# A fixed list of steps for the first chunk of an attention and feed-forward kernel

## The chip, the cores and the metric

One Trainium2 chip, one of its cores. The metric is the device time of one execution in microseconds (us). TensorE (PE; PEld is its weight load), VectorE (DVE), ScalarE (ACT), GpSimd (POOL) and SyncE (SP, which issues all transfers) each run their own queue in order and wait for each other by semaphores.

## What is computed

Local attention with a summary of every block, then a maxout layer, then a bilinear layer:

```python
def _attn_ref(q, k, v):                    # (2, 8, 768, 64)
    block, window = (32, 16)
    k_sum = k.reshape(B, H, nb, block, D).max(axis=3)
    v_sum = v.reshape(B, H, nb, block, D).mean(axis=3)
    scores_l = scale * np.matmul(q, k.transpose(0, 1, 3, 2))   # kept where |i - j| < window
    scores_s = scale * np.einsum('bhsd,bhnd->bhsn', q, k_sum) + np.log(block)
    ...                                    # softmax over both, times [v, v_sum]
def _moe_ref(x, w1, w2, w3, w_out):        # x (1536, 512), d_ff 768
    h = np.maximum(np.maximum(x @ w1, x @ w2), x @ w3)
    return (h @ w_out).astype(np.float32)
def _moe2_ref(x, w_a, w_b, w_out):         # d_ff 1536
    return ((x @ w_a) * (x @ w_b) @ w_out).astype(np.float32)
```

## The kernel before

The 1536 tokens are four chunks of 384 (three tiles of 128). Attention is worked per group `g`: one chunk and one pair of heads `p`, so groups 0 to 3 make chunk 0, groups 4 to 7 make chunk 1. For a group there are, in turn: keys copied into their layout with the block maxima spread between them (`key_parts`, L159); for each of three tiles the scores (`scores`: two products on PE, L251; mask and row minimum on DVE, L257; exponentials on ACT, L258); the normalisation (`normal`: sums to ACT, L273, reciprocal on DVE, L274, scaling on POOL, L276); the transposes of the result (`transposes`: PE L289, out of PSUM by DVE L293 for two tiles and ACT L295 for the third); the values with their block means (`spread`, L180; the means are spread on DVE, L191), turned by PE and copied out by ACT (`turned`, L210 and L211); and the product with the values (`values`, L308), which leaves PSUM split in two halves, a rounded one (ACT, L518) and its rest (DVE, L519). Here this last product of group 3 is called **M3**, its two halves make the fourth slice of chunk 0's `x`.

After that come dense layers: `layers12` multiplies each chunk's `x` with 18 weight tiles (12 products `ph` of 384 columns for each, three products for each of four slices, L514) and so on; `layers34` follows. These products are the bulk of PE's work.

Every 128x512 weight tile, here **w0**, **w1**, ... in the order of loading, comes as 64-bit words and is taken apart by `w_round` and `w_parts`: a scaling `psw` (ACT L444 or DVE L442), the low words (ACT L446), shift and sign (DVE L448, L449), an addition (POOL L450), then a rounded half (ACT L454) and its rest (POOL or DVE, L455). A tile is of use when both halves stand.

What sets the order: SP's transfers go out in program order (its queue is scheduled by hand), eight at most under way, since each waits for the one eight places earlier to land. The other engines' order is set when the program is built, by a scheduler that knows dependencies, priorities and the `issue_after` pins. PE's instructions of the first chunk are pinned one behind the other (`chain`); DVE, ACT and POOL are pinned at a few places only (`behind_all`). `opening` (L317) writes the first chunk's steps, `turn_over` puts products of zeros between them that nothing reads.

Of the kernel before, what the change touches and what calls it, by code (L numbers as in the profile page):

```python
# [19 lines left out]
P = 128  # L20
# [10 lines left out]
NSEG, PAD = S // HALF + 1, HALF - WINDOW  # L31
# [24 lines left out]
W64, W32, WBUFS, QB, FB, SM, GB, BANKS = (4, 3), (4, 3), (24, 10), 4, (9, 1), 2, (12, 9), (2, 2, 1, 2, 2)  # L56
# [7 lines left out]


# [11 lines left out]
def attention_then_maxout_then_bilinear(ctx: ExitStack, tc: tile.TileContext, qt, kt, vt, vwin, wall, const, out):  # L77
# [4 lines left out]
    V, A, G, T = nc.vector, nc.scalar, nc.gpsimd, nc.tensor  # L82
# [67 lines left out]
    def keys(b, p):  # L150

        row = w64_p.tile([P, NSEG * HALF], F32, tag=f"full{b}", name="row", bufs=FB[b])
        nc.sync.dma_start(out=row, in_=kt[b, p][:, P - WINDOW - PAD:])
        if b == 0:
            raw["k", p] = row
        else:
            key_parts(b, p, row)

    def key_parts(b, p, row):  # L159

        kk = k_t[p].rearrange("p (m k) -> p m k", k=SEG)
        row_k = row.rearrange("p (m k) -> p m k", k=HALF)
# [16 lines left out]

    def spread(b, p, full):  # L180

        z = Z_AT[0]
        mean = sm_p.tile([P, 1, NB], F32, tag="mean", name="mean")
        V.tensor_reduce(mean, full.rearrange("p (o n k) -> p o n k", o=1, k=BLOCK), AX.X, ALU.add)
        if b == 0:
            vs = sm_p.tile([P, VSEG, SEG], F32, tag="vs", name="vs")
            G.memset(vs[:, 0, 0:PAD], 0.0)
            G.tensor_copy(vs[:, 0, PAD:HALF], full[:, 0:WINDOW])
            G.tensor_copy(vs[:, 1:VSEG, 0:HALF],
                          full[:, WINDOW:WINDOW + (VSEG - 1) * HALF].rearrange("p (m k) -> p m k", k=HALF))  # L190
            V.tensor_scalar(vs[:, :, HALF:SEG], mean.to_broadcast([P, VSEG, NB]), 1.0 / BLOCK, None, ALU.mult)  # L191
            v_s[p] = vs.rearrange("p m k -> p (m k)")
            return
        ps = ps_t.tile([NB, P], F32, tag="t", name="psvs")
        T.transpose(ps, mean[:, 0], ident)
# [4 lines left out]
    def turned(p):  # L200

        n, vs = SIZES[0], v_s.pop(p)
        for i0 in range(0, n, 2):
            i1 = min(n, i0 + 2)
            ps = ps_t.tile([NC, 2, 2, P], F32, tag="t", name="psvt")
            with chain():
                for i in range(i0, i1):
                    for a in range(2):
                        k0 = (2 * i + a) * SEG + HALF - Z_AT[a]
                        marks["pe"] = T.transpose(ps[:, i - i0, a], vs[:, k0:k0 + NC], ident).ins  # L210
            A.activation(v_t[p][:, i0:i1].rearrange("k i a h d -> k i a (h d)"), ps[:, 0:i1 - i0], AF.Copy)  # L211
# [26 lines left out]
    def scores(g, i):  # L238
# [3 lines left out]
        if i == 0:  # L242
# [5 lines left out]
        with chain(g <= NP) if g <= NP else behind_all("first"):  # L248
# [3 lines left out]
            if g <= NP:  # L252
                marks["pe"] = ins
        for a in range(2):
            mask = cst[:, MASK[t, a]:MASK[t, a] + NC]

            marks["scores", g, i] = V.tensor_tensor_reduce(s[:, a], ps[:, a], mask, -1.0 / D ** 0.5, 3e38, ALU.add, ALU.min, nm[:, a:a + 1]).ins  # L257
            A.activation(s[:, a], s[:, a], AF.Exp, bias=nm[:, a:a + 1], scale=-1.0, accum_out=sm[:, a:a + 1])  # L258
        if g == 0:
            turn_over(TURN[1])  # L260
# [7 lines left out]
    def normal(g):  # L268
# [5 lines left out]
        last[0] = V.reciprocal(r, r).ins  # L274
        s, r = s.rearrange("p i a k -> p (i a) k"), r.rearrange("p i a o -> p (i a) o")
        marks["normal", g] = G.tensor_tensor(s, s, r.to_broadcast([P, 2 * n, NC]), ALU.mult).ins  # L276

    def transposes(g):
        at, n = exps.pop(g)[0], CHUNKS[groups[g][0]][2]
        a_t[g] = aT = sm_p.tile([NC, MAXT, 2, P], F32, tag="aT", name="aT")  # L280
        for i0 in range(0, n, 2):
            i1 = min(n, i0 + 2)
            ps = ps_t.tile([NC, 2, 2, P], F32, tag="t", name="pst")
            if g < NP and i0 == 0:
                turn_over(TURN[2])
# [6 lines left out]
            if AT_DVE[g >= len(groups) // 2][i0 // 2 % 2]:  # L292
                marks["aT", g] = V.tensor_copy(aT[:, i0:i1], ps[:, 0:i1 - i0]).ins  # L293
            else:
                A.activation(aT[:, i0:i1], ps[:, 0:i1 - i0], AF.Copy)  # L295

    def values(g):
# [13 lines left out]
        if g == NP - 1:  # L311
            marks["first"] = ins
        split(x_t[c, p], ps[:, 0:n * P], V)
# [3 lines left out]
    def opening():  # L317

        def spread_(p, i):
# [493 lines left out]
```

## Time and profile before

| | |
|---|---|
| Median of 3 runs | 550.48 us (550.28 to 551.54) |
| The profiled execution | 550.42 us |
| Its span in the trace | 548.6 us |
| PE busy | 538.7 us (98%) |
| DVE, ACT, POOL busy | 384.3, 271.3, 200.4 us |
| Read from HBM | 48.09 MB |

The page gives busy time per engine, the chain of work that ended last, and the costliest groups of instructions. All times in the trace count from the span's start.

### The profile page before, as it was taken

To read this page: it belongs to the slowest core of one execution; us is meant where nothing else is said; L and a number is where in the kernel's file an instruction comes from. 1 tells how busy PE (TensorE), PEld (TensorE's weight loads), DVE (VectorE), ACT (ScalarE), POOL (GpSimd) and SP (SyncE) were. 2 spreads that over 40 slices of the span, in tenths; PEclk is the share of its full clock that TensorE was granted. 3 is DMA by queue.
4 is the path that set the end of the run, shared out by engine and by line. 5 is a ranking of instruction groups with operands and counts; after the bars stand their busy time and mean duration, and the time that the engine had idled before them with its cause. 6 is when DMAs were issued, how large, how long until landed. Compare 5 with 4: busy or idle time off the path is not lost.

```text
span 548.6 us, 8994 instructions
## 1 busy us (share of the span) xinstructions
PE 538.7 (98%) x3364; PEld 513.0 (93%) x3364; DVE 384.3 (70%) x804; ACT 271.3 (49%) x660; POOL 200.4 (37%) x176
## 2 busy tenths in 40 slices
PE   7899999999999999999999999999999999999997
PEld 7789999999999999999999989989998998998986
DVE  5798975785422641739888997986997798574464
ACT  4699765586542422534675545634544542440130
POOL 3479997362210121313414432421621452230120
PEclk9999999999999999999999999999999999999999
DMA  8991831674100002213303042131122121000014
GB/s 306 365 291 73 270 132 67 224 227 129 61 1 1 1 5 111 76 40 116 115 1 115 17 144 72 40 115 58 58 78 76 39 78 39 1 0 1 0 48 184
DMA packets 17131, 51.81 MB, mean 94 GB/s; under 512 B 2112, under 2 KB 2752, under 8 KB 17088
## 3 DMA queue, kind: packets, MB, share of 16 engines
q1 hardware_dynamic: 17088, 51.25, 28.0%
q8 instruction: 26, 0.43, 0.3%
q14 instruction: 17, 0.14, 0.1%
HBM read 48.09 MB, written 3.15 MB: 93 GB/s over the span
## 4 chain that ended last, share of the span: by engine, by line
PE 88%; DVE 5%; issue 1%; ACT 1%; POOL 1%; POOLq 0%; DVEq 0%; ACTq 0%
PE ph L514 24%; PE qb L514 17%; PE qg L514 9%; PE py L514 8%; PE po L683 6%; PE po L684 6%; PE po L682 6%; PE qd L514 4%; PE ps L251 3%; PE psv L308 2%; PE pst L289 2%; DVE wt L455 1%; DVE w L448 1%; POOL t L650 1%; DVE w L449 1%
## 5 line engine op out<-in xcount | busy, mean ns | idle before, releaser
L514 PE MATMUL ph<-x,wt 128*128 128x384 f32 x864 | 156.9, 337 | 0.0
L514 PEld LDWEIGHTS ph<-x,wt 128*128 128x128 f32 x864 | 149.2, 188 | 0.4
L450 POOL TENSOR_TENSOR w<-w,w 128x512 int32<-128x512 int32 x60 | 82.5, 1378 | 161.9 <-DVE w L449 82.8
L514 PE MATMUL qb<-yt,wt 128*128 128x384 f32 x576 | 110.6, 335 | 0.3 <-ACT s L633 0.3
L514 PEld LDWEIGHTS qb<-yt,wt 128*128 128x128 f32 x576 | 101.1, 188 | 1.4 <-ACT s L633 0.6
L518 ACT ACTIVATE hg<-t 128x384 fp32r<-128x384 f32 x72 | 37.0, 521 | 72.1 <-DVE t L542 40.8
L650 POOL TENSOR_TENSOR t<-t,ca 128x384 f32<-128x384 f32 x36 | 44.1, 1241 | 64.4 <-DVE t L649 64.3
L514 PE MATMUL qg<-yt,wt 128*128 128x384 f32 x288 | 58.0, 334 | 0.0
L683 PE MATMUL po<-wt,hg 128*128 128x512 f32 (+1 forms) x146 | 56.6, 387 | 0.0
L684 PE MATMUL po<-wt,hg 128*128 128x512 f32 (+1 forms) x146 | 56.5, 387 | 0.0
L682 PE MATMUL po<-wt,hg 128*128 128x512 f32 (+1 forms) x146 | 56.5, 387 | 0.0
L696 DVE TENSOR_TENSOR acc<-po,acc 128x512 f32<-128x512 f32 (+1 forms) x61 | 40.7, 678 | 21.7 <-PE po L684 21.7
L542 DVE TENSOR_TENSOR t<-ph,t 128x384 f32<-128x384 f32 x48 | 26.4, 552 | 40.2 <-PE ph L514 33.9
L514 PE MATMUL py<-hg,wt 128*128 128x384 f32 x288 | 53.8, 339 | 0.4 <-ACT hg L518 0.4
L514 PEld LDWEIGHTS qg<-yt,wt 128*128 128x128 f32 x288 | 50.7, 188 | 0.0
L514 PEld LDWEIGHTS py<-hg,wt 128*128 128x128 f32 x288 | 49.5, 188 | 0.9 <-ACT hg L518 0.7
L258 ACT ACTIVATE s<-s,nm 128x120 f32<-128x120 f32 x96 | 37.0, 388 | 21.5 <-DVE nm L257 21.0
L444 ACT ACTIVATE w<-w 128x512 f32<-128x512 f32 x30 | 20.2, 675 | 50.6 <-DMA w<-wall 49.6
L454 ACT ACTIVATE wt<-w 128x512 fp32r<-128x512 f32 (+1 forms) x60 | 34.9, 582 | 19.1 <-POOL w L450 9.8
L519 POOL TENSOR_TENSOR hg<-t,hg 128x384 fp32r<-128x384 f32 x23 | 25.0, 1092 | 51.2 <-ACT hg L518 49.0
L446 ACT ACTIVATE w<-w 128x512 int32<-128x512 uint32 x60 | 39.4, 668 | 1.7 <-DMA w<-wall 1.7
L519 DVE TENSOR_TENSOR hg<-t,hg 128x384 fp32r<-128x384 f32 x49 | 36.4, 754 | 2.3 <-ACT hg L518 2.1
(80 smaller groups left out, 786.1 us busy)
## 6 DMA issues: line engine op xcount, KB each, us to landing
w<-wall SPq DMA_DIRECT2D x60, 512.0 KB, 3.5
qv<-qt SPq DMA_DIRECT2D x15, 384.0 KB, 5.8
row<-kt SPq DMA_DIRECT2D x8, 416.0 KB, 4.7
full<-vt SPq DMA_DIRECT2D x8, 384.0 KB, 6.7
out<-acc SPq DMA_DIRECT2D x11, 256.0 KB, 2.0
qv<-vwin SPq DMA_DIRECT2D x12, 192.0 KB, 5.4
qv<-vwin SPq DMA_DIRECT2D x12, 96.0 KB, 5.1
qv<-qt SPq DMA_DIRECT2D x1, 256.0 KB, 4.8
```

What stands on the lines that cost most here:

```text
L258: A.activation(s[:, a], s[:, a], AF.Exp, bias=nm[:, a:a + 1], scale=-1.0, accum_out=sm[:, a:a + 1])
L446: A.activation(lw.bitcast(I32), lw, AF.Copy, scale=2.0 ** -29)
L450: G.tensor_tensor(w.bitcast(I32), w.bitcast(I32), lw.bitcast(I32), ALU.add)
L454: A.activation(w[:, 0], r, AF.Copy)
L514: ins = T.matmul(ps, w[:, i, o:o + P], x[:, j], start=first and n == 0, stop=last and n == 2, skip_group_check=more).ins
L518: A.activation(dst[:, 0], src, AF.Copy)
L519: eng.tensor_tensor(dst[:, 1], src, dst[:, 0], ALU.subtract)
L650: G.tensor_tensor(t, t, cs[c, f], ALU.mult)
L682: T.matmul(ps, g[:, 0], w[:, 0], start=(f == 0), stop=False)
L683: T.matmul(ps, g[:, 0], w[:, 1], start=False, stop=False)
L684: ins = T.matmul(ps, g[:, 1], w[:, 0], start=False, stop=(f == 1)).ins
L696: V.tensor_tensor(acc[c, i][:, cols_], ps, acc[c, i][:, cols_], ALU.add)
```

## The change

The opening is written as a list of 178 small steps, `FIRST`, and while it is worked off the instructions of DVE, ACT and POOL are also pinned one behind the other (`Ordered`), as PE's were. The functions are cut so that each step is one piece for one engine: `key_parts` into copy (`kc`), maxima (`top`) and spreading (`sp`), `scores` into products (`P`), masks (`D`) and exponentials (`E`), `w_round` and `w_parts` into `psw`, `lw`, `sh`, `sg`, `ad`, `hi`, `lo`.

- The scaling `psw` of w0, w1 and w2 is on DVE (before: w1's on DVE, w0's and w2's on ACT). The spreading of the value means (`vp`) is on ACT (before on DVE), four times.
- w0, w1 and w2 are converted within the list, and the first two tiles' 24 products with chunk 0 (`H`) stand in it.
- The order of two loads of q relative to weights and values is another: the list has `q6` and `q7` earlier.
- PE has 29 products of zeros in the opening where it had 33.
- Buffers: raw weight words from the ninth on 4 to 6, converted words 4 to 3, batch 0's raw keys and values 9 to 8, batch 1's 1 to 2.

```diff
-W64, W32, WBUFS, QB, FB, SM, GB, BANKS = (4, 3), (4, 3), (24, 10), 4, (9, 1), 2, (12, 9), (2, 2, 1, 2, 2)
+W64, W32, WBUFS, QB, FB, SM, GB, BANKS = (6, 3), (3, 3), (24, 10), 4, (8, 2), 2, (12, 9), (2, 2, 1, 2, 2)
...
+FIRST = (
+    "top0 kc0 sp0 P00 z2 D00 E00 P02 z2 P01 z2 q4 D02 D01 E02 kc1 top1 E01 sp1 r0 P10 rc0 s0 P11 D10 D11 P12 z2 q5 W4 "
...
+).split()
...
+    class Ordered:
...
+            def call(*args, **kwargs):
+                with behind_all(self.name):
+                    done = getattr(self.engine, op)(*args, **kwargs)
+                marks[self.name] = done.ins
+                return done
...
+    V, A, G, T = Ordered("dve", nc.vector), Ordered("act", nc.scalar), Ordered("pool", nc.gpsimd), nc.tensor
...
-            V.tensor_scalar(vs[:, :, HALF:SEG], mean.to_broadcast([P, VSEG, NB]), 1.0 / BLOCK, None, ALU.mult)
...
+        A.activation(vs[:, :, HALF:SEG], mean.to_broadcast([P, VSEG, NB]), AF.Copy, scale=1.0 / BLOCK)
...
+            if q < OPEN or BIAS_DVE[era(q)][q % 3]:
+                V.tensor_scalar(to, hw.bitcast(F32), 2.0 ** -112, None, ALU.mult)
...
+        pinned[0], done, early = True, {}, {}
+        for step in FIRST:
+            name = step.rstrip("0123456789")
...
+            elif name in ("psw", "lw", "sh", "sg", "ad", "hi", "lo"):
+                w_piece(p, name)
+            elif name == "H":
+                first_products(*at)
...
+        pinned[0] = False
+        w_opened()
...
+    def first_products(n, k):
+
+        if n not in begun:
+            begun[n] = bank("ph")[:, 0:CHUNKS[0][2] * P]
+        with chain():
+            marks["pe"] = mm3(begun[n], w_t[n], k * P, x_t[0, k], k == 0, k == 3)
```

Instructions outside the list are still placed by the scheduler, among the pinned ones where it finds room. Two places of the program that it made:

ACT around M3, before: `w64_144`, `w64_146`, `w64_148` are the raw words of w0, w1 and w2, `x_537` is the rounded half after M3. The three L446 passes are the low words of these three tiles.

```order
L446 ACTIVATE w64_144<-w64_144 128x512
L446 ACTIVATE w64_146<-w64_146 128x512
L446 ACTIVATE w64_148<-w64_148 128x512
L258 ACTIVATE s_443,sm_444<-s_443,nm_446 128x120 x2
L518 ACTIVATE x_453<-psv_454 128x384
L295 ACTIVATE aT_475<-pst_486 120x256
L444 ACTIVATE psw_555<-w64_148 128x512
L454 ACTIVATE wt_522<-w32_511 128x512
L211 ACTIVATE qv_106<-psvt_490 120x512
L211 ACTIVATE qv_106<-psvt_496 120x256
```

ACT at the same place now: `w64_216`, `w64_308` and `w64_409` are the raw words of w3, w4 and w5, `x_492` is the rounded half of the third slice, the two `qv_106<-psvt` copies are group 3's turned values, and `x_552` follows M3.

```order
L115 ACTIVATE wt_524<-w32_456 128x512
L536 ACTIVATE w64_216<-w64_216 128x512
L536 ACTIVATE w64_308<-w64_308 128x512
L536 ACTIVATE w64_409<-w64_409 128x512
L525 ACTIVATE psw_603<-w64_216 128x512
L115 ACTIVATE x_492<-psv_493 128x384
L115 ACTIVATE qv_106<-psvt_528 120x512
L115 ACTIVATE qv_106<-psvt_534 120x256
L115 ACTIVATE w64_148<-w64_148 128x512
L115 ACTIVATE x_552<-psv_553 128x384
```

Three low-word passes that are not in the list, of w3, w4 and w5, and w3's scaling now stand ahead of the third slice's split and of group 3's turned values; the pass over w5 waits for w5's transfer.

SP's queue, before: `qv_106<-qt` (L221) are the loads q6 and q7, `w64_299`, `w64_386` and `w64_388` are w4, w5 and w6, `vwin` are values.

```order
L234 DMA qv_106<-vwin 32x768
L234 DMA qv_106<-vwin 64x768
L424 DMA w64_299<-wall 128x512
L221 DMA qv_106<-qt 128x768
L234 DMA qv_106<-vwin 32x768
L234 DMA qv_106<-vwin 64x768
L424 DMA w64_386<-wall 128x512
L424 DMA w64_388<-wall 128x512
L221 DMA qv_106<-qt 128x768
```

SP's queue now, from q6 on (it is the row ahead of the first of these): `w64_308`, `w64_409` and `w64_411` are w4, w5 and w6.

```order
L286 DMA qv_106<-vwin 32x768
L286 DMA qv_106<-vwin 64x768
L501 DMA w64_308<-wall 128x512
L273 DMA qv_106<-qt 128x768
L286 DMA qv_106<-vwin 32x768
L286 DMA qv_106<-vwin 64x768
L501 DMA w64_409<-wall 128x512
L501 DMA w64_411<-wall 128x512
```

q6 moved ahead of w4 and of two loads of values, and q7 moved ahead of w5: both now stand in front of w5.

PE up to M3 (`psv_553`) and just past it, now: `ph_516` and `ph_544` are the products of w0 and w1, `pst_591` is the first transposed piece of group 4.

```order
L626 MATMUL ph_516<-x_292,wt_449 128x384 x3
L262 MATMUL psvt_528<-kept_105,vs_383 120x128 x4
L262 MATMUL psvt_534<-kept_105,vs_383 120x128 x2
L626 MATMUL ph_516<-x_391,wt_449 128x384 x3
L626 MATMUL ph_544<-x_292,wt_524 128x384 x3
L358 MATMUL pst_591<-kept_105,s_431 120x128 x4
L383 MATMUL psv_553<-aT_477,qv_106 64x64 x12
L626 MATMUL ph_544<-x_391,wt_524 128x384 x3
```

Before, M3 had one such product `ph` in front of it and no transpose of group 4; now it has nine and four. The 30 products of scores ahead of it are the same number in both.

## Rows read from the trace of the kernel before

**Rows 1.** The page, part 1: busy us and share of each engine.
```profile
PE 538.7 (98%) x3364; PEld 513.0 (93%) x3364; DVE 384.3 (70%) x804; ACT 271.3 (49%) x660; POOL 200.4 (37%) x176
```
**Rows 2.** Chain that ended last, 28 to 70 us: start us, us, what.
```profile
28.18 0.59 DVE psw L442
28.77 1.18 DVE w L448 x2
29.95 1.20 DVE w L449 x2
31.15 0.61 DVE aT L293
31.80 1.15 PE ps L251 x8
...
33.28 0.92 PE psv L308 x24
...
63.41 6.67 PE ph L514 x37
```
**Rows 3.** Stretches of the opening: us, busy (instructions) per engine, PEclk, DMA share, GB/s.
```profile
6.45:14.20 7.75, 5.93 (x49) 5.45 (x48) 5.95 (x28) 4.96 (x23) 4.65 (x8) 1.00 1.03 399
14.20:30.00 15.80, 13.03 (x153) 11.48 (x152) 12.48 (x48) 11.90 (x45) 6.88 (x12) 1.00 1.04 344
```
**Rows 4.** Groups on ACT, 0 to 60 us: xcount | busy us, mean ns | idle before.
```profile
L258 ACT ACTIVATE s<-s,nm 128x120 f32<-128x120 f32 x48 | 18.5, 390 | 9.9 <-DVE nm L257 9.5 <-ACT r L273 0.5
...
L446 ACT ACTIVATE w<-w 128x512 int32<-128x512 uint32 x12 | 7.6, 676 | 0.0
...
L444 ACT ACTIVATE psw<-w 128x512 f32<-128x512 f32 x8 | 5.1, 637 | 0.1
L518 ACT ACTIVATE x<-psv 128x384 fp32r<-128x384 f32 x7 | 3.4, 479 | 0.0
L295 ACT ACTIVATE aT<-pst 120x256 f32<-120x256 f32 x8 | 3.0, 380 | 0.7 <-PE pst L289 0.7
L211 ACT ACTIVATE qv<-psvt 120x512 f32<-120x512 f32 x4 | 2.3, 580 | 0.5 <-PE psvt L210 0.5
L273 ACT ACTIVATE r<-sm 128x6 f32<-128x6 f32 x8 | 1.7, 206 | 0.1
```
**Rows 5.** Groups on DVE, 0 to 60 us.
```profile
L257 DVE CUSTOM_DVE_ANT_0 s<-ps,kept 128x120 f32<-128x120 f32 x48 | 11.3, 275 | 3.9 <-PE ps L251 3.7
L448 DVE TENSOR_SCALAR w<-psw 128x512 uint32<-128x512 uint32 x11 | 7.4, 683 | 0.0
...
L519 DVE TENSOR_TENSOR x<-psv,x 128x384 fp32r<-128x384 f32 x7 | 3.8, 548 | 0.0
...
L191 DVE TENSOR_SCALAR vs<-mean 128x168 f32<-128x168 f32 x4 | 1.8, 446 | 0.0
```
**Rows 6.** The transfer of w5 alone: its issue on SP, and issue to landing.
```profile
L424 SPq DMA_DIRECT2D w<-wall x1: 523/523/523, 24.3 to 24.3; - x1
...
DMA to landing us min/median/max: 8.1/8.1/8.1
```
**Rows 7.** Two stretches, columns as in rows 3; the transfers' rate stands last.
```profile
5.00:21.40 16.40, 13.39 (x119) 11.54 (x117) 11.79 (x50) 9.47 (x42) 8.75 (x17) 1.00 1.02 396
21.40:32.40 11.00, 9.15 (x105) 7.98 (x106) 9.61 (x32) 9.79 (x35) 4.39 (x4) 1.00 1.04 312
```
**Rows 8.** Timeline of PE: start us, us, operation, [idle before it].
```profile
1.05 4.22 PE L266 MATMUL idle<-zeros 128*128 128x128 f32 x22 [1.05 <-DVE zeros L716]
...
10.76 1.06 PE L266 MATMUL idle<-zeros 128*128 128x128 f32 x8
...
22.34 0.92 PE L308 MATMUL psv<-aT,qv 120*64 120x64 f32 x24 [0.96 <-ACT qv L211]
```

More of the change, by code (lines that the diff above doesn't have):

```diff
@@ L198, in spread, with value_words, value_copy, value_means @@
                      AF.Copy, scale=1.0 / BLOCK)
[L200 to L211, printed above, removed]
+    def value_words(p):
+        if p not in v_s:
+            v_s[p] = sm_p.tile([P, VSEG, SEG], F32, tag="vs", name="vs")
+        return v_s[p]
+    def value_copy(p):
+        full = raw["v", p]
+        vs = value_words(p)
+        G.memset(vs[:, 0, 0:PAD], 0.0)
+        G.tensor_copy(vs[:, 0, PAD:HALF], full[:, 0:WINDOW])
+        G.tensor_copy(vs[:, 1:VSEG, 0:HALF],
+                      full[:, WINDOW:WINDOW + (VSEG - 1) * HALF].rearrange("p (m k) -> p m k", k=HALF))
+    def value_means(p, mean):
+        vs = value_words(p)
+        A.activation(vs[:, :, HALF:SEG], mean.to_broadcast([P, VSEG, NB]), AF.Copy, scale=1.0 / BLOCK)
+    def turned(p, i0):
+        i1 = min(SIZES[0], i0 + 2)
+        vs = v_s[p].rearrange("p m k -> p (m k)")
+        ps = ps_t.tile([NC, 2, 2, P], F32, tag="t", name="psvt")
+        with chain():
+            for i in range(i0, i1):
+                for a in range(2):
+                    k0 = (2 * i + a) * SEG + HALF - Z_AT[a]
+                    marks["pe"] = T.transpose(ps[:, i - i0, a], vs[:, k0:k0 + NC], ident).ins
+        return lambda: A.activation(v_t[p][:, i0:i1].rearrange("k i a h d -> k i a (h d)"), ps[:, 0:i1 - i0], AF.Copy)
     def load(g):
@@ L317, in opening @@
     def opening():
-        def spread_(p, i):
-            with behind_all(("scores", min(p + 1, NP - 1), i)):
-                spread(0, p, raw["v", p])
         for p in range(NP):
@@ L351, in opening @@
-        spread_(NP - 1, 2)
-        g = NP
-        scores(g, 0)
-        values(g - 2)
-        load_values(g - 2 + NP)
-        w_ask(ASKS[4])
-        transposes(g - 1)
-        behind = last[:]
-        turned(g - 1)
-        scores(g, 1)
-        more(behind)
-        scores(g, 2)
-        normal(g)
-        values(g - 1)
-        load_values(g - 1 + NP)
-        more(behind)
-    def more(behind):
-        with tc.issue_after(behind[0]), tc.issue_after(behind[1]):
-            weights(1)
+        pinned[0], done, early = True, {}, {}
@@ L430, in w_ask @@
             w_at[0] += 1
[L432 to L450 removed]
+    words = {}
@@ L495, in weights @@
                     w_at[n] += 1
-    late = []
+    late, begun = [], {}
+    def first_products(n, k):
+        if n not in begun:
+            begun[n] = bank("ph")[:, 0:CHUNKS[0][2] * P]
+        with chain():
+            marks["pe"] = mm3(begun[n], w_t[n], k * P, x_t[0, k], k == 0, k == 3)
     def flush():
@@ L531, in layers12 @@
                 hs[f] = hg_p.tile([P, 2, MAXT * P], F32R, tag="hg", name="hg")
-            ps = bank("ph")[:, 0:n_]
-            for k in range(4):
-                mm3(ps, w_t[n], k * P, x_t[c, k], k == 0, k == 3)
+            if c == 0 and n in begun:
+                ps = begun[n]
+            else:
+                ps = bank("ph")[:, 0:n_]
+                for k in range(4):
+                    mm3(ps, w_t[n], k * P, x_t[c, k], k == 0, k == 3)
             flush()
```

230 lines of the change are left out of this document (143 added, 87 removed), and 6 rows, old and new, of the table FIRST.

## The prediction

> **What bounds the kernel now.** I read the page's busy times first, then the chain of waits, then the opening in stretches, then what ACT, DVE and the transfers do there. On the page PE is busy for 538.7 of the span's 548.6 us, far ahead of DVE's 384.3 [rows 1]. The chain says from when that holds: up to 31.8 us its pieces change between engines (among them, just ahead, 3.0 us of weight conversion on DVE: 0.59 + 1.18 + 1.20, then a copy out of PSUM of 0.61), and from 31.80 us on it is PE's own work; from 63.41 us 37 products in a row take 6.67 us, 0.18 us each [rows 2]. So the run is an opening that PE spends mostly waiting, and then a block of PE work of fixed size. Nothing that happens on other engines later counts unless it makes PE wait. The change can give or take only one thing: when that block gets going, measured with the work already done by then.
>
> In the opening the other engines are full or waiting for each other. ACT is busy 4.96 of the 7.75 us after its first exponential (6.45 us) and 11.90 of the next 15.80 us, so it idles 2.8 and 3.9 us [rows 3]. The transfers are never idle: their share stays above 1.00 from 5.0 to 32.4 us, at 396 GB/s up to 21.4 and at 312 GB/s after it [rows 7]. What comes later in SP's queue lands later; w5, issued at 24.3, lands 8.1 us on, at 32.4 us [rows 6].
>
> **The yardstick.** I take M3, since it needs nearly everything of the opening. It starts at 33.28 us [rows 2]. With the change PE has by then done eight more products (8 x 0.18 = 1.44 us) and four transposes of 128 columns, which I price as the products of zeros of that size, 1.06 us for eight [rows 8], so 4 x 0.13 = 0.5 us. M3 may therefore start at 33.28 + 1.94 = 35.2 us at no change in the total. Each microsecond earlier or later is one gained or lost, as long as PE does not wait behind it.
>
> **The change part by part.**
>
> Conversion out of the way: the 3.0 us on DVE that stand in front of group 3's copy [rows 2] are spread over times in which DVE would wait. This is the gain that the list can bring, and what it comes to depends on what is late next.
>
> Late next is ACT, because of three passes that are not in the list. ACT works in order; behind w1's rounded half now stand the low words of w3, w4 and w5, then w3's scaling, then the third slice's split, then group 3's turned values, which M3 reads. The pass over w5 can't begin before w5 has landed, and all of ACT's queue stands behind it. So two times matter.
>
> (a) When ACT arrives there. In front are 30 exponentials, at 18.5 us for 48 (0.385 each) 11.6 us; five sums 1.05; four spreadings of means, 4 x 0.39 = 1.6; three copies of 512 columns 3 x 0.58 = 1.7 and seven of 256 columns 7 x 0.38 = 2.7; two splits of x 1.0; four passes over low words 4 x 0.63 = 2.5; two rounded halves, as the scaling of that size, 1.3 [rows 4]. Together 23.4 us, from 6.45 us on: 29.9 with no wait. Short instructions overlap by some 0.1 us at their ends (a mean of 676 ns against 7.6 us for 12), which takes off about 2 us: 27.9. Of the idle time the 2.8 us up to 14.2 us stay in any case, since they are waits for the first transfers: 30.7 us. With all 6.7 us of idle time kept it would be 34.6. I take 30.7, since the steps that made the later 3.9 us are now interleaved with other work.
>
> (b) When w5 lands. Before: 32.4 us. Its transfer now has one more ahead, q7 (384 KB, 0.393 MB): at 396 GB/s 0.99 us, at 312 GB/s 1.26 us [rows 7]. The slower rate is that of this very stretch, so 33.7 us; the bounds are 33.4 with q7 at the faster rate, and 31.1 if all of it, 11.0 us at 312 GB/s and q7, went at 396. Issuing early doesn't help: SP has eight under way.
>
> The later of the two decides: 33.7 us. From there low words 0.63, scaling 0.64, split 0.49, copy of 512 columns 0.58 [rows 4] make 36.0 us, the four transposes, which wait for that copy's bank, 0.5: M3 starts at 36.5 us. That is 36.5 - 35.2 = 1.3 us **later** than at no change. ACT's own arrival at 34.6 would make it 2.2 us; q7 at the faster rate makes it 1.0.
>
> Behind M3 DVE is late next. It stood still for want of the third split (ready about 35.3 us) and then has ten weight passes and copies of 0.68, three masks of two halves at most 0.75 each, two rests of x and one maximum at 0.55 each: 10.7 us at most, so to 46.0, less some 0.1 us overlap for each, about 44.5 [rows 5]. The piece it ends with is asked for by w3's first product. PE gets there from 36.5 with M3 and group 4's product, 2 x 0.92, 15 and 12 products of 0.18, two transposes and six score steps of at most 0.6, at about 46.5. No wait, with a microsecond or two to spare.
>
> The swaps of the title: w0's and w2's scaling move to DVE, 2 x 0.68 = +1.4 us there and 2 x 0.64 = -1.3 us on ACT; four spreadings of means leave DVE, 4 x 0.446 = -1.8 us, and go to ACT. A copy of 7x24 means is not in the trace on ACT; it lies between the 206 ns of six columns and the 390 ns of an exponential over 120 [rows 4], and I take the latter, as it is a copy of 168: +1.6 us (0.8 at the least). Net +0.3 on ACT, -0.4 on DVE. ACT waits for w5 anyway, which covers its part; without that cover it costs 0.3.
>
> The 24 early products fill time in which PE waits, and are counted in the yardstick as far as they stand ahead of M3. Four fewer products of zeros (0.13 each) lie in PE's waits: nothing. q6 moved past w4 and values: they are used only after 40 us, nothing. Buffers: more raw words of later weights can be under way, but PE never waits for weights after 63 us; three converted words instead of four could hold DVE for a rest that is late, with the slack above as cover. Below nothing and above 0.4 us for these; I take nothing.
>
> Sum against the profiled execution, 550.42 us (0.06 below the median): 550.4 + 1.3 = **551.7 us**. The main case reaches from 1.0 to 2.2, so 551.4 to 552.6.
>
> **The rivals.**
>
> *The clock falls while PE waits.* For: the products before M3 end by about 32 us (w1's second half is ready soon after ACT's first pass of the three begins), and the next piece needs the copy at 36.0: a wait of some 4 us, where the longest of PE's waits now, once it has begun, is 0.96 us or so [rows 8]. The trace shows what PE does after standing still: 22 products of zeros take 4.22 us at the start, 0.19 each, and 0.13 each later [rows 8]. I read the slower pace as the lower of TensorE's two levels, 1.2 and 2.4 GHz, though the granted clock reads 1.00 in the stretches shown [rows 3]. Against: the wait may be shorter, by as much as ACT's arrival or w1's products are later than I make them. Price: 4.22 us of work at the start's pace instead of the later one costs 4.22 x (1 - 0.13/0.19) = 1.3 us, at exactly half the clock 2.1 us. It gives 551.7 + 1.7 = 553.4, **slower**. It decides once the clock really drops, whatever the wait's length.
>
> The Trainium skill, page "TensorE: Matmul & The Clock Gate", section "Part 1: The HAM clock gate (the "warmup" mystery)", says "the default state is throttled, and activity releases the throttle", and its section "HAM oscillation" tells of kernels that pay this at each long wait. By that rule the sum would be 553.4 and not 551.7. No wait of such length is in this trace, so it can neither bear the rule out here nor speak against it.
>
> *The transfer is early enough.* The slow stretch may belong to the order of transfers before (values among them) and not to its time. At 396 GB/s w5 is there at 31.1 us, M3 at 33.9: 1.3 us earlier than the yardstick, 549.1 us. If it never holds ACT, M3 comes at 30.7 + 2.8 = 33.5: 1.7 us gained, 548.7. Against: q7 is in front, and the rate is below 320 GB/s over eleven microseconds. If w5 lands as before, at 32.4, the result is 550.4.
>
> **How the numbers follow.** 0.3% is 1.65 us, about what a measurement of this kernel can tell from no change: the bounds are 548.8 and 552.1 us. Main case (551.4 to 552.6) 0.54, of which 0.40 within the bounds and 0.14 above. Clock falls (553.0 to 554.2) 0.24, slower. Transfer early (548.7 to 550.4) 0.18, of which 0.08 faster and 0.10 within. Some wait on DVE or POOL behind M3 that I don't see (above 553) 0.04, slower. So faster 0.08, same 0.50, slower 0.42. For 8 in 10 the range runs from 549.4, which leaves out half of the early transfers, to 554.0, which leaves out the last case and the end of the clock's.
>
> **What would show it.** Right: in the changed profile ACT has an idle time of 2 to 3 us that ends with the landing of a `w`, at 33 to 34 us, ahead of a low-words pass; DVE and PE are idle for about 4 us at the same time; M3 starts at 36 to 37 us; from there PE runs through. The clock's rival: products of 384 columns just after that wait at about twice 0.18 us. Wrong: M3 before 35 us, no wait of ACT for a weight, or waits of PE after 45 us that the old trace hasn't.

## The result, and the profile after

The changed kernel takes 557.58 us (median of 4 runs, 555.78 to 558.82) against 550.44 of the kernel before: 1.0123 times, with a 95% interval of 1.0092 to 1.0154. It is **slower**, and outside the predicted range of 549.4 to 554.0. The profiled execution is the fastest of the four (555.78 us, span 554.0, before 548.6).

PE's busy time on the page is little changed against [rows 1], but it is not the same work: it holds eight fewer instructions and a stretch at half the clock.

```profile
PE 539.8 (97%) x3356; PEld 513.8 (93%) x3356; DVE 387.8 (70%) x804; ACT 270.9 (49%) x662; POOL 198.1 (36%) x174
```

ACT's timeline around the landing of w5 (start, us, operation, [idle before it and what ended it]):

```profile
30.64 1.25 ACT L536 ACTIVATE w<-w 128x512 int32<-128x512 uint32 x2
33.42 0.65 ACT L536 ACTIVATE w<-w 128x512 int32<-128x512 uint32 x1 [1.53 <-DMA w<-wall]
33.98 0.60 ACT L525 ACTIVATE psw<-w 128x512 f32<-128x512 f32 x1
34.52 0.47 ACT L115 ACTIVATE x<-psv 128x384 fp32r<-128x384 f32 x1
34.89 0.86 ACT L115 ACTIVATE qv<-psvt 120x512 f32<-120x512 f32 x2
```

The pass over w5's low words (L536) waits 1.53 us for its transfer, and w3's scaling, the third split and group 3's turned values stand behind it. The transfer itself, as in [rows 6]: issued at 25.1, 8.3 us on the way, there at 33.4 us.

```profile
L501 SPq DMA_DIRECT2D w<-wall x1: 337/337/337, 25.1 to 25.1; - x1
...
DMA to landing us min/median/max: 8.3/8.3/8.3
```

PE's timeline in the same place. `psv` x24 at 36.63 is M3, which stood at 33.28 in [rows 2]:

```profile
32.72 0.62 PE L626 MATMUL ph<-x,wt 128*128 128x384 f32 x2 [0.70 <-DVE wt L115]
35.62 1.08 PE L358 MATMUL pst<-kept,s 128*120 128x128 f32 x4 [2.28 <-ACT qv L115]
36.63 1.55 PE L383 MATMUL psv<-aT,qv 120*64 120x64 f32 x24
38.11 3.25 PE L626 MATMUL ph<-x,wt 128*128 128x384 f32 x9
41.15 0.63 PE L358 MATMUL pst<-kept,s 128*120 128x128 f32 x2
41.57 1.22 PE L303 MATMUL ps<-kept,qv 128*128 128x120 f32 x8
```

M3 lasts 1.55 us instead of 0.92, and nine products of 384 columns 3.25 us, 0.32 us from start to start, where [rows 2] have 0.18. The stretches (columns as in [rows 3]; PEclk is the first number behind POOL) say why:

```profile
30.00:35.00 5.00, 2.64 (x15) 1.95 (x15) 2.66 (x4) 3.47 (x8) 1.39 (x1) 1.00 1.04 286
35.00:38.00 3.00, 2.38 (x28) 2.06 (x28) 2.98 (x6) 1.33 (x3) 0.00 (x0) 0.52 0.93 284
38.00:41.50 3.50, 3.50 (x15) 3.29 (x12) 1.78 (x4) 0.49 (x1) 2.54 (x2) 0.50 0.61 178
41.50:45.00 3.50, 3.50 (x44) 3.25 (x42) 2.62 (x15) 3.18 (x11) 0.00 (x0) 0.94 0.89 316
...
55.00:60.00 5.00, 4.68 (x46) 3.80 (x44) 4.41 (x8) 4.78 (x18) 3.81 (x3) 1.00 0.00 0
60.00:65.00 5.00, 4.82 (x45) 4.51 (x46) 4.62 (x10) 3.87 (x9) 5.00 (x6) 1.00 0.12 24
65.00:70.00 5.00, 4.63 (x48) 4.21 (x47) 4.74 (x8) 2.55 (x6) 5.00 (x4) 1.00 0.60 210
70.00:80.00 10.00, 9.78 (x56) 9.78 (x57) 8.74 (x14) 7.14 (x15) 9.28 (x8) 1.00 0.70 229
```

PE stood 0.70 and then 2.28 us; the granted clock, 1.00 until then, is 0.52 and 0.50 in the next two stretches, the level of 1.2 GHz instead of 2.4, and by the 0.94 of the stretch behind them it is back at about 41.9 us, an estimate. And between 55 and 80 us PE stands still for 0.32 + 0.18 + 0.37 + 0.22 = 1.1 us. Before, it was full there; two of the four stretches:

```profile
55.00:60.00 5.00, 5.00 (x51) 4.67 (x50) 4.81 (x9) 4.52 (x10) 5.00 (x6) 1.00 0.84 315
...
70.00:80.00 10.00, 10.00 (x60) 10.00 (x59) 6.98 (x12) 7.56 (x15) 10.00 (x9) 1.00 0.31 108
```

The chain of waits leaves PE in this place and goes over the conversion of a weight (start, us, what):

```profile
52.38 1.21 DVE wt L560
...
57.58 1.30 POOL w L545
58.88 1.26 POOL wt L560
...
60.18 2.52 PE ph L626 x13
...
69.68 0.50 ACT x L630
```

**Where 5.3 us went.** PE begins `layers34` (its first `qb`) at 231.69 us before and at 236.96 now, 5.27 later; behind that the two run alike (313.7 us each to PE's end). PE's timelines, before and now:

```profile
231.69 0.85 PE L514 MATMUL qb<-yt,wt 128*128 128x384 f32 x4
```

```profile
236.96 0.85 PE L626 MATMUL qb<-yt,wt 128*128 128x384 f32 x4
```

M3 comes 36.63 - 35.2 = 1.4 us behind the prediction's yardstick; 0.46 of that is the transposes ahead of it at half clock (1.08 instead of 0.62 us), so w5's wait makes 1.0. This is net: in e1_lw5last below, where w5 does not hold ACT, M3 comes at 34.33, 0.9 us ahead of the yardstick, so the wait itself costs about 1.8 us and eats the 0.9 that the list gains. The clock makes 0.46 + 0.63 (M3) + 1.40 (nine products) + 0.25 + 0.17 (the next two rows) = 2.9, by the same rows of e1_lw5last below. Late waits make 1.1 and 0.3 more at 118 us. Sum 5.3. This is the profiled execution; the median of the four is 1.8 us longer, and no trace shows what that part is.

### The profile page after: what moved, and what is told of

Same layout as the page of the kernel before. It is cut to its first block, busy times and chain, and to the rows that moved or that the text cites. A ratio compares the mean times of both kernels' runs of the same rounds, so it can differ in the third digit from the quotient of the medians.

```text
span 554.0 us, 8999 instructions
## 1 busy us (share of the span) xinstructions
PE 539.8 (97%) x3356; PEld 513.8 (93%) x3356; DVE 387.8 (70%) x804; ACT 270.9 (49%) x662; POOL 198.1 (36%) x174
## 4 chain that ended last, share of the span: by engine, by line
PE 88%; DMA 4%; DVE 4%; ACT 1%; POOL 1%; issue 1%; SPq 0%; DVEq 0%; POOLq 0%
PE ph L626 25%; PE qb L626 18%; PE qg L626 9%; PE py L626 8%; PE po L798 6%; PE po L797 6%; PE po L799 6%; PE qd L626 5%; DMA w<-wall 3%; PE ps L303 2%; PE psv L383 2%; PE pst L358 1%; DMA full<-vt 1%; PE idle L327 1%; DVE wt L560 1%
## 5 line engine op out<-in xcount | busy, mean ns | idle before, releaser
L626 PE MATMUL ph<-x,wt 128*128 128x384 f32 x864 | 159.2, 339 | 2.1 <-DVE wt L115 0.7
L545 POOL TENSOR_TENSOR w<-w,w 128x512 int32<-128x512 int32 x57 | 77.7, 1365 | 161.3 <-DVE w L542 67.3
L657 DVE TENSOR_TENSOR t<-ph,t 128x384 f32<-128x384 f32 x48 | 26.5, 552 | 39.2 <-PE ph L626 30.7
L631 POOL TENSOR_TENSOR hg<-t,hg 128x384 fp32r<-128x384 f32 x23 | 25.7, 1119 | 49.5 <-ACT hg L630 49.5
L559 ACT ACTIVATE wt<-w 128x512 fp32r<-128x512 f32 (+1 forms) x57 | 32.9, 580 | 10.1 <-POOL w L545 10.1
L536 ACT ACTIVATE w<-w 128x512 int32<-128x512 uint32 x57 | 37.1, 668 | 1.5 <-DMA w<-wall 1.5
L560 DVE TENSOR_TENSOR wt<-w,wt 128x512 fp32r<-128x512 f32 (+1 forms) x43 | 31.3, 729 | 2.9 <-ACT wt L559 2.9
```

The source lines that it names most:

```text
L536: A.activation(lw.bitcast(I32), lw, AF.Copy, scale=2.0 ** -29)
L545: G.tensor_tensor(w, w, lw.bitcast(I32), ALU.add)
L559: A.activation(w[:, 0], r, AF.Copy)
L560: eng.tensor_tensor(w[:, 1], r, w[:, 0], ALU.subtract)
L626: ins = T.matmul(ps, w[:, i, o:o + P], x[:, j], start=first and n == 0, stop=last and n == 2, skip_group_check=more).ins
L631: eng.tensor_tensor(dst[:, 1], src, dst[:, 0], ALU.subtract)
```

## Experiments

My theory: ACT, held by w5's transfer, makes M3 late; PE's wait lets the clock fall; late waits follow. The rival: three buffers for converted words and the new order of DVE and POOL cost the time, and w5 nothing. The table has, from the traces, w5's landing, M3, the first product of `layers34`, and the median of the runs, all in us.

| run | w5 lands | M3 | layers34 | median |
|---|---|---|---|---|
| before | 32.4 | 33.28 | 231.69 | 550.4 |
| after | 33.4 | 36.63 | 236.96 | 557.6 |
| e0_bufs4 (control) | 35.1 | 37.96 | 241.30 | 560.6 |
| e1_lw5last | 34.9 | 34.33 | 233.53 | 552.0 |
| e2_w5early | 34.3 | 37.07 | 239.46 | 559.3 |
| e3b_warm | 33.2 | 38.15 | 234.76 | 557.1 |
| e9_fewer_steps | 34.6 | 33.91 | 230.15 | 549.4 |
| e11_late_fewer | 36.2 | 39.39 | 236.25 | 556.3 |
| e12_warm_short | 35.5 | 38.36 | 237.51 | 560.1 |
| b1_words3 | 34.4 | 33.21 | 232.33 | 551.2 |

### Is it w5?

**e0_bufs4**, the control, since the other edits need room in SBUF:

```diff
-W64, W32, ... = (6, 3), (3, 3), ...
+W64, W32, ... = (4, 3), (3, 3), ...
```

> The changed kernel with four buffers for raw weight words instead of six, which leaves room for the other edits; it is their control. Mine: the loads up to w5 keep their times (w5 lands at 33.4 us within 0.3), group 3's product with values starts at 36.6 within 0.3, products run at half clock behind it, total 557.6 within 1.5 us. Rival (the six buffers and the loads that they let begin are what costs): 2 us or more below the changed kernel.

Measured: 560.63 us (560.08 to 561.96), 1.0186 times before [1.0168 to 1.0204], 3 us above the changed kernel, where I had expected no change. w5 landed 1.7 us later than there, though nothing ahead of it was edited. And a second stall stands at 71 us: with four buffers the next raw words are asked for only at 63.9 us (in the changed kernel two more weights had gone out at 41), and now DVE stands in order behind a transfer, x's rest behind it, and PE behind that. DVE's and PE's timelines:

```profile
70.44 0.70 DVE L523 TENSOR_SCALAR psw<-w 128x512 f32<-128x512 f32 x1 [1.78 <-DMA w<-wall]
```

```profile
74.24 2.06 PE L626 MATMUL ph<-x,wt 128*128 128x384 f32 x8 [2.68 <-DVE x L631]
```

So six buffers were no loss, the opposite: the rival's form for the raw words falls.

**e1_lw5last** takes w5's pass alone out of ACT's way:

```diff
-            A.activation(lw.bitcast(I32), lw, AF.Copy, scale=2.0 ** -29)
+            with behind_all("act") if q == 5 else ExitStack():
+                A.activation(lw.bitcast(I32), lw, AF.Copy, scale=2.0 ** -29)
```

> Four raw-word buffers, and ACT's pass over w5's low words alone stands behind the last ACT step of the list, so that ACT reaches group 3's x and turned values without waiting for w5. Mine (ACT held by w5's transfer, then PE's wait, then the clock): group 3's product with values starts at 34.3 to 35.2 us instead of 36.6; PE's wait ahead of it shrinks from 2.4 us to about 1; if the granted clock then stays at 1.00 the total is 1.5 + 2.7 = about 4 us below the control, if it falls all the same 1.5 us below. Rival (the loss is in three buffers for converted words and in the order of DVE and POOL, not in w5): within 0.8 us of the control.

Measured: 552.02 us, 1.0019 [1.0007 to 1.0030], 8.6 below the control. PE's timeline:

```profile
33.08 0.61 PE L627 MATMUL ph<-x,wt 128*128 128x384 f32 x2 [0.70 <-DVE wt L115]
33.78 0.62 PE L358 MATMUL pst<-kept,s 128*120 128x128 f32 x4
34.33 0.92 PE L383 MATMUL psv<-aT,qv 120*64 120x64 f32 x24
35.18 1.85 PE L627 MATMUL ph<-x,wt 128*128 128x384 f32 x9
36.87 0.38 PE L358 MATMUL pst<-kept,s 128*120 128x128 f32 x2
37.09 1.05 PE L303 MATMUL ps<-kept,qv 128*128 128x120 f32 x8
```

w5 lands at 34.9, behind M3, and nobody minds. The wait of 2.28 us is gone, the granted clock reads 1.00 in every stretch, the nine products take 1.85 us. One line in one place removes most of the control's loss: the order of ACT's queue around w5 is what costs. The gain is twice what I expected, since the stall at 71 us went too. With the changed kernel's six raw buffers the line was not tried alone; e10_best below, which has it and two moved scalings, is 5.0 us under the changed kernel.

**e2_w5early** puts the loads q6 and q7 back in SP's order:

```diff
-... P22 q6 r1 E20 rc1 M0 u0 W5 top3 ... z2 q7 vcb1 ... M1 z2 u1 W7 vm3 ...
+... P22 r1 E20 rc1 M0 u0 W5 q6 top3 ... z2 vcb1 ... M1 z2 u1 W7 q7 vm3 ...
```

> Four raw-word buffers, and the transfers of the q slices 6 and 7 go back to their places of before in SP's queue, so that w5 is asked for with one transfer less ahead; ACT's order as in the changed kernel. Mine: w5 lands at 32.2 to 32.5 us instead of 33.4, group 3's product with values starts 0.9 to 1.2 us earlier, and the total falls by that much if the clock still drops, by 3 to 4 us if the shorter wait keeps it up. Rival (w5's landing is not what holds): within 0.8 us of the control.

Measured: 559.34 us, 1.0157 [1.0124 to 1.0190]. w5 came 0.8 us earlier than in the control and M3 0.9, as expected, but at 34.3 us and not at 32.4: in this execution it was issued at 25.7 us and 8.6 us on the way, where [rows 6] have 24.3 and 8.1. The total fell by 1.3 us with overlapping intervals, so this run settles little by itself. With the others it gives a rule of the changed order: M3 starts 2.8 to 3.2 us behind w5's landing (33.4 and 36.63; 35.1 and 37.96; 34.3 and 37.07; 36.2 and 39.39). In the kernel before there is none: w5 at 32.4 or, in b1_words3, 34.4, M3 at 33.2 or 33.3 both times.

### Is it the clock?

**e3_warm** and **e3b_warm** put products of zeros into PE's two waits and leave w5 late. Both also have (9, 1) buffers for raw keys and values, where the control has (8, 2). The first:

```diff
-... lo1 H01 vca3 xl2 H10 vcb3 ...
+... lo1 H01 y4 vca3 xl2 H10 y9 y2 vcb3 ...
+            elif name == "y":
+                spare = ps_s.tile([P, 2, NC], F32, tag="s", name="spare")
+                for _ in range(p):
+                    with chain():
+                        marks["pe"] = T.matmul(spare[:, 0], zeros, zeros[:, 0:NC], start=True, stop=True).ins
```

> Four raw-word buffers, and 15 products of zeros of 128 columns into a spare PSUM bank stand in PE's two waits ahead of group 3's product with values (4 ahead of the second piece of the first products, 11 behind it); w5 is as late as before. This prices the clock by itself. Mine: the granted clock stays at 1.00 from 35 to 42 us, group 3's product still starts at 36.6 within 0.4, its 24 pieces take 1.5 us and the first products behind it 0.18 us each instead of 0.32, and the total falls by 2.7 us (2 to 3.4). Rival (the slow products come from something else, such as operands that are late, or the clock falls whatever PE does there): half pace remains and the total is within 0.8 us of the control.

Measured: 559.17 us, 1.0150 [1.0122 to 1.0177]. It does not tell the two apart: the last two products had a bank of their own, and that was late, so PE still stood 2.31 us and the clock fell (0.58 from 38 to 41.5 us). e3b_warm has one bank for all, and `y6`, then `y9 y9 y2`:

> As e3_warm, but the products of zeros (6 ahead of the second piece of the first products, 20 behind it) all go into one bank, so that they wait for nothing; control is e0_bufs4. Mine: PE's longest wait ahead of group 3's product is under 1.2 us, the granted clock stays at 1.00 from 35 to 45 us and the first products behind it start every 0.18 us, and what the clock cost there, 2 to 3 us, is gone, although w5 still lands as late and group 3's product starts as late. Rival (the slow products come from something else than PE's wait): half pace remains, no gain.

Measured: 557.06 us (556.16 to 557.32), 1.0113 [1.0095 to 1.0131], 3.6 below the control. PE's timeline, then the stretches:

```profile
33.60 4.62 PE L445 MATMUL spare<-zeros 128*128 128x120 f32 x40
38.15 0.92 PE L383 MATMUL psv<-aT,qv 120*64 120x64 f32 x24
39.00 1.84 PE L632 MATMUL ph<-x,wt 128*128 128x384 f32 x9
```

```profile
35.00:38.00 3.00, 3.00 (x29) 3.00 (x28) 3.00 (x6) 1.67 (x4) 0.55 (x1) 1.00 0.87 283
38.00:41.50 3.50, 3.50 (x43) 3.28 (x43) 3.05 (x5) 1.83 (x4) 3.44 (x4) 1.00 0.28 76
```

M3 is 0.2 us later than in the control, here held by the zeros themselves (twice the products that I had counted on). Yet products run at 0.18 us from start to start, the clock never leaves 1.00, and `layers34` begins 6.5 us earlier. The waits at 60 and 70 us are gone as well. So the slow products come from PE's wait, not from late operands. The 6.5 us are not the first fall alone: behind M3 that costs the control 0.63 (M3) and 0.76 us (nine products in 2.61 instead of 1.85 us). The waits at 60, 70 and 71 us (3.8 us) and a second fall behind them make the rest. Some 3 us are lost again behind 300 us, where this build waits for ACT (`qb` for `u`, 1.1 us); I have not tried whether its (9, 1) buffers are the reason.

**e12_warm_short** halves the zeros (`y3`, then `y9 y1`):

> As e3b_warm with half the products of zeros: there the second block of them ran 4.62 us (twice the products counted on, since each one of them shows as two) and was itself what group 3's product waited for. Here they should end about when group 3's values are ready. Mine: the clock stays at 1.00, w5 still holds ACT, group 3's product starts 2.8 to 3.3 us behind w5's landing, about 36 us where w5 lands at 33.3, and no waits of PE over 0.5 us between 45 and 120; then the total is what the prediction's main case gave, 551.5 to 554, some 7 us below the control e0_bufs4. Rival (filling PE's wait moves the loss elsewhere): 556 or more.

Measured: 560.12 us, 1.0159 [1.0142 to 1.0176]. It did not become the case I wanted: w5 landed at 35.5, the zeros were over at 35.4, PE stood 2.31 us more, and the clock fell to 0.51. A second fall came at 290 us behind a wait for ACT, so this total says nothing about the opening. The rule above is confirmed (M3 2.9 us behind the landing). ACT's timeline, then PE's:

```profile
35.48 0.67 ACT L542 ACTIVATE w<-w 128x512 int32<-128x512 uint32 x1 [3.80 <-DMA w<-wall]
```

```profile
38.36 1.55 PE L383 MATMUL psv<-aT,qv 120*64 120x64 f32 x24
39.84 2.57 PE L632 MATMUL ph<-x,wt 128*128 128x384 f32 x9
```

Up to `layers34` the trace does tell something. This kernel is e3b_warm with fewer zeros, M3 starts only 0.2 us later, and `layers34` starts 2.75 us later: 0.2 for M3, 0.63 and 0.73 us for M3 and nine products at the low clock, and two waits of 0.64 and 0.79 us at 120 and 133 us (3.0 by these rows). So a fall of the clock, all else nearly equal, cost 1.4 us behind M3 here; in the changed kernel, where more work ran at half clock, the rows behind M3 make 2.45 us. And between 55 and 80 us PE does not wait here either, although the clock fell.

The price of w5's wait alone, with the clock up and no zeros in the way, was thus not measured in one trace.

### What is late behind M3?

**e9_fewer_steps** leaves out three of seven conversion steps of w6 to w11, on top of e1_lw5last:

```diff
+        if 6 <= q < 12 and name in ("lw", "sg", "ad"):
+            return
```

> e1_lw5last without three of the seven conversion steps (low words, sign, sum) of w6 to w11; those weights are therefore only roughly theirs, and ACT, DVE and POOL have 6 x 0.63, 6 x 0.68 and 6 x 1.3 us less to do. Mine (what e1_lw5last still loses against before is PE waiting for converted weights between 54 and 120 us, 2.4 us): those waits go and the total falls by 1.5 to 2.6 us, to 549.4 to 550.5, below the kernel before. Rival (PE's late waits have other causes: scores, x, masks): within 0.8 us of e1_lw5last.

Measured: 549.41 us (548.93 to 550.11), 0.9969 [0.9955 to 0.9983]. The stretch from 55 to 60 us, of e1_lw5last and of this run:

```profile
55.00:60.00 5.00, 4.66 (x46) 4.00 (x45) 4.58 (x9) 4.29 (x10) 4.95 (x5) 1.00 0.22 60
```

```profile
55.00:60.00 5.00, 5.00 (x52) 4.72 (x50) 4.96 (x9) 3.81 (x9) 3.06 (x3) 1.00 0.82 290
```

PE is full again from there on. So behind M3 the conversion work on ACT, DVE and POOL was what PE waited for. Not always as a weight: the waits that the traces name end with the rest of a weight (0.50 us in the changed kernel), but also with x (0.59 us there) and with scores, x and a maximum on ACT and DVE (0.2 to 0.3 us each in e1_lw5last), which stand in the same queues. With M3 at 33.91, 35.2 - 33.9 = 1.3 us ahead of the yardstick, `layers34` comes 1.5 us earlier than before and the runs are 1.25 us shorter (before had 550.66 beside them): once nothing waits, the list is worth what the yardstick says. This kernel leaves out work, though, so that gain can't be had this way.

**e11_late_fewer**: the same omission in the control, where w5 still holds ACT.

> e0_bufs4 (w5 holds ACT, the clock falls) without three of the seven conversion steps of w6 to w11, as in e9_fewer_steps. Mine: group 3's product is as late as in the control and products run at half clock for 2 to 5 us behind it, but the waits at 60, 70 and 71 us (0.6, 0.9 and 2.8 us) go, and with them the second fall of the clock, so that the total is 4.5 to 6 us below the control, 554.5 to 556; what is left above before, some 4 to 5.5 us, is the late product and the clock. Rival (those late waits follow from w5 and the clock, not from the conversion): within 1.5 us of the control, 559 to 561.

Measured: 556.25 us (551.89 to 558.06), 1.0083 [1.0060 to 1.0106], 4.4 below the control. w5 landed later than in any other run, PE stood 5.06 us, products ran at half clock behind it, and still there is no late wait and no second fall. PE's timeline, and its stretch from 55 us on:

```profile
38.38 1.08 PE L358 MATMUL pst<-kept,s 128*120 128x128 f32 x4 [5.06 <-ACT qv L115]
```

```profile
55.00:60.00 5.00, 5.00 (x51) 4.68 (x51) 4.93 (x14) 4.92 (x17) 4.84 (x4) 1.00 0.46 130
```

So late product and clock on one side and late waits on the other are separate parts of the loss. The gain is at the lower edge of what I expected. Two of the ten runs took 551.9 us, with a mean granted clock of 1.000; the other eight took 553.6 to 558.1 us at 0.993 to 0.997. So where the clock did not fall this kernel, with w5 in ACT's queue, took some 4 us less, 2.5 us more than e9_fewer_steps; these two runs have no trace, so when w5 landed in them is not known. What the late waits need is open in one point: e3b_warm and e12_warm_short have none at 55 to 80 us without any omission, one with the clock at 1.00 and one with a fall. They share M3 at 38.2 to 38.4 us, which the control has too (37.96), and they share the products of zeros and the (9, 1) buffers, which it has not.

Four runs tried to mend the supply in e1_lw5last. For room three of them have fewer buffers for raw keys and values, (7, 2) in e4_words4 and (8, 1) in e7_bufs5 and e10_best, instead of (8, 2); the expectations call these the feed-forward's rows. **e4_words4** has four buffers for converted words, `(4, 3), (4, 3)`:

> e1_lw5last with four buffers for converted words, as before the change, instead of three (and one less for the rows of the feed-forward, to make room). Mine: the waits of PE that are left behind the opening (0.2 to 0.5 us each at 54 to 65 and at 110 to 118 us, 2.4 us in all) shrink by at least 1 us, and the total is 1 to 2.5 us below e1_lw5last, 549.5 to 551. Rival (the third buffer isn't what they wait for; DVE and POOL are simply later with the list): within 0.6 us of e1_lw5last.

Measured: 552.96 us, 1.0048 [1.0033 to 1.0063], not faster, and in the traced execution the clock fell once behind a wait at 64 us. The four runs with a mean clock of 1.000 are no faster either, 552.2 to 553.0 us. The third buffer isn't what is short. **e7_bufs5** has five for raw words, `(5, 3), (3, 3)`:

> e1_lw5last with five buffers for raw words instead of four (one less for the feed-forward's rows, to make room). Mine: the next raw words are asked for about 3 us earlier than at 57.9 us, ACT's wait for them ahead of 63 us goes, and 0.3 to 1 us of PE's waits behind 59 us with it: 551 to 551.7. Rival (the engines' time for converting is what is short, not words to convert): within 0.4 us of e1_lw5last.

Measured: 550.60 us, 0.9992 [0.9981 to 1.0004], 1.4 below e1_lw5last. **e8_psw_dve** moves two scalings:

```diff
-            if q < OPEN or BIAS_DVE[era(q)][q % 3]:
+            if q < OPEN or q in (6, 8) or BIAS_DVE[era(q)][q % 3]:
```

> e1_lw5last with the scaling of w6's and w8's words on VectorE instead of ScalarE, which is full from 38 to 57 us. Mine (behind group 3 the supply of converted weights is short and ACT is its tightest engine): the rests of w6 and w7 end earlier than 55.2 and 60.1 us and the total falls by 0.3 to 1 us. Rival (DVE or POOL is the tightest, DVE loses what ACT gains): no gain, or up to 1 us slower.

Measured: 550.56 us, 0.9990 [0.9978 to 1.0003], 1.5 below: the seventh and the eighth rest of a weight end at 53.4 and 57.8 instead of 55.2 and 60.1 us. Both gains are somewhat larger than expected. **e10_best** has the moved scalings and six raw buffers:

> e1_lw5last with both of the edits that gained: the scaling of w6's and w8's words on VectorE, and six buffers for raw words, as in the changed kernel (one less for the feed-forward's rows). Mine: group 3's product stays at 34 us, PE's late waits shrink to under 1 us in all, and the kernel is 0.5 to 1.5 us below before, 549.2 to 550.2; the floor is e9_fewer_steps, 549.4. Rival (both edits give the same time, not one each): 550.6, no difference from before.

Measured: 552.56 us (551.44 to 556.03), 1.0046 [1.0026 to 1.0067]: a miss. The gains don't add, and against e8_psw_dve two raw buffers more (and one fewer for keys and values) cost 2 us; PE waits 0.7 us for ACT, 0.5 for POOL and 0.5 for DVE behind 45 us. The number of raw buffers also sets how far ahead the loads stand in the program, which may change the order of the engines behind them; which order is good stays open. No version beats the kernel before: e7_bufs5 and e8_psw_dve equal it.

### The parts by themselves

The prediction and the expectations call the moves of `psw` and of the means the swaps of the title. **e6_unswap** is e1_lw5last with `psw` of w0 and w2 back on ACT and the spread of the means back on DVE:

> e1_lw5last with the two swaps of the title undone inside the list: ScalarE scales w0's and w2's words again, VectorE spreads the means. Mine: ACT is the chain of waits from 37 to 52 us in e1_lw5last, but the swapped work lies ahead of 34 us, where the list interleaves it; within 0.8 us of e1_lw5last (552.0). Rival (the swaps cost 2 us here too, as in b2_swaps): 549.5 to 550.5.

Measured: 551.50 us, 1.0012 [0.9993 to 1.0032]: no difference from e1_lw5last that can be told. **b1_words3**, **b2_swaps** and **b3_psw_dve** are the kernel before with one edit each: `W32 = (3, 3)`; the two swaps; e8's scalings on DVE.

> The kernel before with three buffers for converted words instead of four and nothing else. Mine: PE gets waits of a few tenths behind 50 us and the total rises by 0.5 to 2 us. Rival (three suffice, as the prediction took it): within 0.6 us of the kernel before.

Measured: 551.21 us, 1.0008 [0.9999 to 1.0018]: at most 1 us, between the two expectations.

> The kernel before with the two swaps of the title alone: VectorE takes the scaling of the first three weights' words, ScalarE the spread of the means. Mine: ACT and DVE trade about as much, the total stays within 0.8 us of before. Rival (a spread on ACT that comes in its order behind exponentials makes the turned values late, or DVE's further passes do): 1 us or more slower.

Measured: 552.74 us, 1.0037 [1.0023 to 1.0051], 2 us slower, the rival's side: in the old order the third rest, on DVE, comes at 42.5 us (before 40.1), and PE waits 0.97 us for it (ahead of that it waits 0.8 us for a copy by DVE, in front of the turning of the values):

```profile
42.55 2.20 PE L514 MATMUL ph<-x,wt 128*128 128x384 f32 x11 [0.97 <-DVE wt L455]
```

> The kernel before with the scaling of w6's and w8's words on VectorE. Mine: before, PE does not wait for weights behind 34 us, so it gains nothing: within 0.5 us of before. Rival (that step is simply better placed there, list or no list): 0.8 us or more faster.

Measured: 553.81 us, 1.0068 [1.0041 to 1.0094], 3 us slower, which neither theory expected; its trace shows new waits of PE for ACT at 63 us and for DVE at 128 us. The same move gains 1.5 us in one order and loses 3 in another.

## Why the prediction was wrong

- **The bound and the yardstick: right.** 35.2 us for "no change" was borne out where nothing waited behind M3: e9_fewer_steps (M3 1.3 us ahead of it, `layers34` 1.5 earlier) and e3b_warm (M3 3.0 behind it, `layers34` 3.1 later). In e11_late_fewer it is less exact: M3 4.2 behind it and 1.2 us of slow work behind M3, `layers34` 4.6 later.
- **(a) ACT's arrival:** 30.7 us forecast, 31.9 measured (the two passes from 30.64 on). Still ahead of w5, so without consequence, as said, but ACT's idle time was 1.53 us and not 2 to 3. The overlap of 0.1 us for each instruction does not follow from its row: 12 x 0.676 - 7.6 us, over 12, is 0.04.
- **(b) w5's landing:** 33.7 forecast, 33.4 in the changed kernel. But I took it as a fixed number. Over the runs that keep the changed order of loads it is 33.2 to 36.2 us, and M3 follows where ACT waits for w5. The changed kernel's runs spread over 3 us where before spread over 1.3, and their median is 1.8 us above the profiled one. That w5 makes this spread is not shown: e1_lw5last, with w5 out of the way, spreads over 2.6 us.
- **M3:** 36.5 forecast, 36.6 measured, in part by luck: 0.46 us of it is the transposes at half clock, which the sum did not have, and w5 came 0.3 earlier. The size of the wait was off (2.3 and 0.7 us, not 4 in one), since w1's second half came late from DVE.
- **The steps that failed** are two terms that the sum has at nothing. The larger is what follows PE's wait: the main case let PE stand for some 4 us and then go on at full pace, and the clock was left to a rival. It cost 2.9 us (next point but one). With it and the 1.4 us of late waits the traced execution comes to 550.4 + 1.0 + 2.9 + 1.4 = 555.7 us, where the sum has 551.7.
- **The second of them** is "No wait, with a microsecond or two to spare". I followed DVE only to w3's first product, and there it is right: the fourth rest stands at 46.3 us, and the chain has 24 products in a row from 46.7 us on. The shortage shows with later weights, at 59 to 70 us, which is one of the prediction's own signs of being wrong. Its case of a wait on DVE or POOL behind M3 had 0.04. POOL, which converts them too, did nothing at all from 35 to 38 and from 41.5 to 45 us. The words "Nothing that happens on other engines later counts unless it makes PE wait" were true, and I then did not go on to ask. The same goes for buffers priced at nothing: four raw buffers instead of six cost 3 us in the changed order, five instead of four gain 1.4 in e1_lw5last's.
- **The clock's rival was the case that came**, with 0.24. Its mechanism was right: products at 0.32 us behind the wait, none of it where the wait is gone or filled. Its price of 1.7 us measured 2.9. I took as the slow stretch the 4.22 us of the start, at a pace short of half; here PE worked at half the clock for some 6 us (35.6 to 41.9). The Trainium skill's rule cited for it (page "TensorE: Matmul & The Clock Gate", section "HAM oscillation") holds at this wait, the 0.50 to 0.52 of 35 to 41.5 us beside it; not every long wait was followed by a fall, as the last section shows. Main case, clock and late waits were also taken as alternatives; they came together: 1.0 + 2.9 + 1.4 us.
- **The swaps:** nothing forecast, nothing within the list (e6_unswap), 2 us in the old order (b2_swaps).

## What to carry to other kernels

When engines run a fixed order, look at each instruction that waits for a transfer and ask what stands behind it in its queue; put it behind all work that does not need that transfer, or each late landing holds up that work too. Price a wait of PE as the wait plus the slow work that may follow it, and follow the next supply past the first place where it holds. A move that helps in one order can cost as much in another, so measure it in the order it is meant for.

## What was not expected of the hardware

The length of one wait does not decide whether the clock falls. The closest pair is e0_bufs4 and e2_w5early, whose orders differ by two loads: behind 69 us PE waits 0.67 and 2.68 us in the one, 0.66 and 2.66 us in the other, ahead of the same products. In the first the granted clock is 0.50 from 76 to 78 us, in the second it stays at 1.00. Their stretches, e0_bufs4 first:

```profile
76.00:78.00 2.00, 2.00 (x7) 2.00 (x7) 0.47 (x1) 2.00 (x5) 1.44 (x2) 0.50 0.37 96
```

```profile
76.00:78.00 2.00, 2.00 (x14) 2.00 (x13) 1.24 (x3) 2.00 (x5) 0.87 (x2) 1.00 0.76 256
```

A shorter wait can be followed by a fall: in e4_words4 PE stood 1.73 us and ran at 0.50 from 67 us on. PE's timelines of e4_words4, with a stretch behind it, and of e2_w5early:

```profile
65.99 2.23 PE L627 MATMUL ph<-x,wt 128*128 128x384 f32 x8 [1.73 <-DVE x L632]
```

```profile
67.00:68.00 1.00, 1.00 (x4) 1.00 (x4) 1.00 (x1) 1.00 (x3) 0.75 (x1) 0.50 0.91 311
```

```profile
73.48 1.83 PE L626 MATMUL ph<-x,wt 128*128 128x384 f32 x9 [2.66 <-DVE x L631]
```

The Trainium skill, same page, section "Part 1: The HAM clock gate (the "warmup" mystery)", says of the clock's rise behind a start that its point differs from run to run. No trace here shows a rise in two executions of one kernel; for the fall, e11_late_fewer's ten runs of one program, two at a mean granted clock of 1.000 and eight below, show such a difference. And the same weight, issued in the same place of the queue, landed up to 3 us apart in different executions (33.2 to 36.2 us), issued at 25.1 to 27.2 us and 7.9 to 9.6 us on the way.
